# First-MLP tiles evicted in pairs from one bank, short score parts of two queries' blocks in shared banks, and a new order behind job 60

## The chip, the cores and the metric

The kernel runs on one core of a Trainium2 chip. The metric is the device time of one execution in microseconds (us); of several runs the median is given. The engines are TensorE (PE; its weight loads are shown as PEld), VectorE (DVE), ScalarE (ACT), GpSimd (POOL) and SyncE (SP, which here only issues DMAs). Matmuls write to PSUM, which has 8 banks of 512 fp32 values in each of 128 partitions.

## What is computed

Two branches are added to the input x of 2048 tokens by 512, both on the layer-normed x.

```
xn = layernorm(x)                          # 2048 x 512
# branch A: 32 heads of 16, 4 segments of 512 tokens
logits = q k^T / 4 + mask                  # within a segment
a_dot  = softmax(logits) v
a_mem  = (phi(q) M) / (phi(q) z + 1e-6)    # phi(t) = t+1 if t>0 else exp(t)
o      = g a_mem + (1-g) a_dot             # g = sigmoid(beta), per head
M, z  += phi(k)^T v, sum phi(k)            # for the next segment
A = o wo
# branch B: MLP with 1792 hidden units
B = gelu(layernorm(xn) w1 + b1) w2 + b2
out = x + A + B
```

## The kernel before

**Jobs.** The work is cut into some 1300 jobs. Each is a Python call that emits its instructions on all engines that it needs; an engine works through its own instructions in the order in which the jobs are emitted. `streams()` lists the jobs of each kind in their own fixed order; the string `ORDER` has one letter a job and says from which stream the next job comes. So `ORDER` fixes the order of every engine's queue, the DMA queue of SP included. It was made outside of this file. The string `BANKS` has one digit for each PSUM tile, in the order in which the jobs ask for them: `dense()` takes the next digit and returns that bank whole (128 x 512 fp32). Semaphores between the engines follow from the tiles: who takes a bank waits for the last reader of its earlier content.

**Groups.** A group i (0 to 15) is one segment of 512 tokens and 8 heads. Its jobs are:

- `T` (L495): q or k projected, 12 matmuls of 128x512; the halves are written to DRAM and read back in another layout (qst, kst).
- `M` (L636, L643): row maxima of the scores. For each t of 4 (two heads each) and each query block of 128 there are scores of up to 512 keys in two banks, one for each of two heads, by pairs of matmuls on the two halves of the array (48 rows each). VectorE adds the mask and takes the maximum straight from PSUM, one reduction and one read of its accumulator for each bank and block. The parts of a t are: block 3 (512 keys), blocks 2 and 0 (384 and 128 in one bank), block 1 (256). Each part is a job: 12 for a group.
- `R` (L514, L653 to L659): the maxima are transposed, split into halves of fp16, written to DRAM (md) and read back as two more rows of qst.
- `S` (L676, L681, L690): scores again, transposed, with the maximum taken off by these rows (50 rows); ScalarE takes exp from PSUM, POOL masks the diagonal blocks.
- `pv`, `PV` (L705): probabilities times v, with 32 columns of the array each, four at a time; `O` (L729 to L741) normalizes in three steps, over DVE, ACT and POOL.
- `N`, `K`, `Z`, `Qd`, `Q`: the memory branch (transposes of phi(k), products with v, phi(q) times the memory, its normalization).

**MLP.** It is cut into 16 jobs' worth j: 256 tokens (half hf of a segment) by one half of the hidden units (fh, 7 tiles of 128). `D` (L495 with w1s, L771): one tile of 128 hidden units by 256 tokens, 12 matmuls, then one VectorE instruction that scales it by a column and by a row `srow` into hT. `G` (L778): gelu of all seven tiles, on ScalarE, after a load of its table. `H` (L785 to L787): splits them into halves of fp16. `e` (L812, L818): the second layer, 14 jobs of 6 matmuls on the halves of the array, into two banks. `out` (L830, L833): the output projection of 128 tokens.

`V` projects v, `X` and `Xt` are the layer norm and its transposes, `wl`, `wm`, `wf` and `ws` load, measure, scale and split the weights in the first 80 us, `warm` (L843) is 8 matmuls of no use that keep PE busy; there are 14.

The names that the prediction speaks of are written with their indices: T(1,0) is q of group 1, S(7,3,1) the second score job of t = 3 of group 7, Q(15) the normalization of group 15's memory part, H(15,3) the last split of MLP job 15.

Of the kernel before, what the change touches and what calls it, by code (L numbers as in the profile page):

```python
# [14 lines left out]
OP = mybir.AluOpType  # L15
# [4 lines left out]
P = 128  # L20
D = 512
KT = D // P
# [9 lines left out]
FH = FT // 2  # L32
# [69 lines left out]


ORDER = (
    "atacctcaetcttetcawvavcatwvcaxeacatxvdccwvxwfttyyyxbxyyuxgyyyzozoywouoxyccyzhoAzzAootAAppciiizAznpBiiABfBncAiBpi"
    "gzBszniipnzBiimchqqqiCBqBqiiioAoACBCCBCjjqiojqAjqjcioijoiCikskkBcmDskioBjiqiqCjjoijqCiqjsCqjDiftaoCCpgkkkpkjqCj"
    "oloojjljoloojiipkkkkiqihspqijqqipqijqiqjsjqqjaajfgpiiqkkkkmpliqqiooiqpDlqoDopohijjiojiijpolsjiqaqajqiqiqqiiqapk"
    "akmkktspaqijqiqjqiqajqbqajopijjgDfopkkkDkjjjlooooDlhjjjolqiqqiipkkkkjiqqijqqjjiqiqjjqiqiqiDkkkkmpliilfnplimpngr"
    "rmrjjponijqjqjinjipiskmkkmkaiijrijjoojiqsjqqjiqiiiqqkkkkihlqlfmlogojqjqjqqjjasoojmkkkkmqjiqjqjjaojjpipmooisikkk"
    "klpilhiofmgoooqiqpppqiqiqqqiiiqqpsosmoiqqiiqiqppsslooijqjojijojijoiaakkkkmpaijqjqjaqqqjiqqjiqjqiikmkkakbqiaqqah"  # L110
    "lolfqjjojqmjgjjoolmmkkkkmhjjoojjiitjiojiippkkkkliiilnfnimpligniinipmrrijjrsijqjqiqjiqjqiipkmkkksiqjqijqjqjiqjqi"
    "iqjqikmpkkkiprlqsphlfojmjgopjjlojpjoomokmkkkqiqisjojiqisjqiqijqqijqhiqqiiqjsqiiqppmkkkkilalofomqpgopaoooospmlaj"
    "qqqjqqjqjqiiqiqqqjqiqqipipooooiijooppoiaakkkkmajiqpisqqjiqjqjaiqaqhjqqqjqaaqmkkkkbjlfoljqjmjgojjqolmkkkkmmjjjoo"
    "jjioijoiiippkpkkkiinliifniiilnnimlgrpmjjrmjjjrrijikkpskkiqqijqiqijqqjiqjiqjqiqjiqiispqkpkskksqilqoplfojmjgjjjpo"
    "ooojolmkkkkiqjiqpsjiqiqijqjqiqijqjiqiqiqiiqqkksmkpikplolfjjqmjgjjjoooooklpkmkkjiiopjqiqijqjiqpjqiqijqiqqiqiiqik"
    "kpspkkqiplpoooopljjjqqqjqjjqooolkpskmkpkmqqqpqjpjqqqjqjqpqqjqjqqqkmkkkqlllqqqqqqqqqrrrr"
)

BANKS = (
    "050123614061756123401632157467410534702651305176254301741260523716405142730612547306651240651024615024612504612"
    "504650124650412650412650412650142650142650421607653420107642531076425031702531270531270531270132570132570132576"
    "135402761350427163054273106542736574326574326537425632754632574631072456310724563071245360712453620731620731067"
    "203617621073621073621073621037621037621037261702361475023671540263701524603175246031746013746013713460713471630"
    "471630463714067314056723410523674105236741052367410527410527410527410527410527140352671450326475103264751023674"
    "523674523647253647236547236475264735264107532410765324107265431067512043675120436751204736152047361520473615270"
    "346150312750317250317253107250371257013275027135027134650132754062751340621375460376054370567403056374065374065"
    "307645307645307642153076241076241076241076253410762534621075346210754316024310264310432610432610324610324612403"
    "246013752640163754207156437120564371205647312056473120564731206547321065473265104723607423460273460273642073642"  # L130
    "073642051736420157642031765420316750316705315631705630157630157630157306173504621357462017345620147536210436024"
    "136024316403216403216403216403216740536740536740536740536271406"
)


# [14 lines left out]
def infini_mixer_kernel(ctx: ExitStack, tc: tile.TileContext, x, wq, wk, wv, wo, beta, w1, b1, w2, b2, out):  # L150
# [15 lines left out]
    def dense():  # L166
        return dps.tile([P, 512], F32, name="ps" + next(bank), bufs=1)
# [52 lines left out]
    def col(j):  # L220
        return sc[:, j:j + 1]
# [210 lines left out]
    srow = {}  # L432
# [192 lines left out]
    mc = cst.tile([P, 96], F32, name="mc")  # L625

    def m_jobs(i):
        def f(t, qbs):
            def go():
                ps = dense(), dense()  # L630
                o = 0
                for qb in qbs:
                    n = P * (qb + 1)
                    for b, p in enumerate(ps):
                        r = slice(64 * b, 64 * b + KM)
                        T.matmul(p[:, o:o + n], stk[i, 0][r, t, P * qb:P * qb + P], stk[i, 1][r, t, :n],  # L636
                                 start=True, stop=True)
                    o += n
                o = 0
                for qb in qbs:  # L640
                    n = P * (qb + 1)
                    for b, p in enumerate(ps):
                        V.tensor_tensor_reduce(p[:, o:o + n], p[:, o:o + n], mask[:, 512 - n:], 1.0, -3e38,  # L643
                                               OP.add, OP.max, mc[:, 16 * b + 4 * t + qb:16 * b + 4 * t + qb + 1])
# [114 lines left out]
    def d_jobs(j):  # L759
        hf, fh = divmod(j, 2)  # L760
        hs, hh = divmod(hf, 2)
        own = slice(256 * hh, 256 * hh + 256)
        hz = hzs[fh]

        def f(fi):
            def go():
                fo = FH * fh + fi
                p = dense()
                split3(p[:, :256], ((WT["1"], lambda w, k, a: w[:, fo, a, P * k:P * k + P]),
                                    (xnT[hs], lambda t, k, a: t[:, k, a, own])), KT, True, True)  # L770
                V.scalar_tensor_tensor(hz[:, fi, :], p[:, :256], col(F1 + fh), srow[hs][:, own], op0=OP.mult, op1=OP.mult)  # L771
            return go
        return [f(fi) for fi in range(FH)]

    def gelu(j):
        for f in range(FH):
# [149 lines left out]
```

## Time and profile before

| | before |
|---|---|
| median of 3 runs | 691.06 us (690.85 to 691.38) |
| the profiled execution | 691.51 us |
| its span, first to last instruction | 689.8 us |
| granted TensorE clock | 0.999 |

A profile line of a group reads: line of the kernel, engine, operation, output <- inputs, shape, count | busy us, mean ns of one | idle us before it, and what ended that. Matmuls are pipelined: the record of one runs on while the next has begun, so PE's idle time shows only where it was longer than this. In the chain that ended last, each piece is followed back from the last instruction to what released it.

The shape of a matmul line is rows*columns of the array that it uses, then the output. 128*128 is the whole array; 48*128, 50*128 and 64*128 are one of its halves; 128*32 is a quarter of its columns.

### The profile page before, as it was taken

The page shows a single profiled execution, that of the slowest core. Times are in us where ns is not written, and L with a number is a line of the kernel's source. Part 1 is how long each engine was busy: PE and PEld are TensorE (multiplying, and loading weights), DVE is VectorE, ACT ScalarE, POOL GpSimd, SP SyncE. Part 2 cuts the span into 40 slices and gives each one's busy share as a digit, 9 for nine tenths or more (in the row PEclk, how much of TensorE's full clock was granted, in tenths as well). Part 3 has the DMA queues.
Part 4 walks back from the last instruction along what each step waited for, and adds up shares of the span by engine and source line. Part 5 has one row for each costly group of instructions (what it writes and reads, how often), then busy time and mean ns, then how long its engine had stood idle before and what let it go on. Part 6 is the DMA issues. An engine that isn't in the chain of part 4 may idle for free.

```text
span 689.8 us, 17163 instructions
## 1 busy us (share of the span) xinstructions
PE 681.8 (99%) x6465; PEld 399.8 (58%) x6465; DVE 545.7 (79%) x1740; ACT 502.9 (73%) x972; POOL 340.5 (49%) x526
## 2 busy tenths in 40 slices
PE   8999999999999999999999999999999999999997
PEld 7855655565654546566554557567564456656653
DVE  6999968897795887998797787888688696969442
ACT  4486897788786659856794796766795687878870
POOL 5355567456535334663435355454353545446752
PEclk9999999999999999999999999999999999999999
DMA  9856342421203322421213224231120415140101
GB/s 277 249 149 201 92 109 49 117 55 31 65 24 102 94 67 45 122 50 33 69 26 98 58 73 100 72 86 32 41 72 24 132 19 154 17 109 2 19 1 62
DMA packets 51792, 55.15 MB, mean 80 GB/s; under 512 B 4782, under 2 KB 40636, under 8 KB 51708
## 3 DMA queue, kind: packets, MB, share of 16 engines
q1 hardware_dynamic: 49404, 49.84, 24.9%
q0 software_dynamic: 2304, 4.20, 3.8%
q8 instruction: 51, 0.84, 0.5%
q14 instruction: 33, 0.27, 0.1%
HBM read 36.99 MB, written 17.04 MB: 78 GB/s over the span
## 4 chain that ended last, share of the span: by engine, by line
PE 85%; DVE 5%; ACT 5%; DMA 2%; POOL 1%; issue 1%; SPq 0%; POOLq 0%; DVEq 0%; ACTq 0%
PE ps L495 36%; PE ps L812 17%; PE ps L705 10%; PE ps L830 6%; PE ps L676 5%; PE ps L636 5%; DVE ps L643 3%; ACT pt L681 2%; PE ps L586 2%; PE ps L514 1%; PE ps L843 1%; PE ps L321 1%; DMA wks<-in_A_wk_dram 1%; DMA qd<-hl 1%; PE ps L617 1%
## 5 line engine op out<-in xcount | busy, mean ns | idle before, releaser
L643 DVE CUSTOM_DVE_ANT_0 ps<-ps,mask 128x512 f32<-128x512 f32 (+3 forms) x512 | 233.9, 523 | 14.1 <-PE ps L636 12.9
L681 ACT ACTIVATE pt<-ps,qkcs 128x512 f32<-128x512 f32 (+1 forms) x384 | 206.8, 624 | 37.3 <-PE ps L676 35.2
L812 PE MATMUL ps<-w2s,hT 64*128 64x512 f16 x1344 | 176.6, 375 | 0.1
L495 PE MATMUL ps<-xnT,w1s 128*128 128x256 f16 x1344 | 158.0, 273 | 0.0
L690 POOL TENSOR_SCALAR_AFFINE_SELECT pt<-pt 128x256 f32<-128x256 f32 x256 | 101.0, 421 | 98.2 <-ACT pt L681 97.2
L495 PEld LDWEIGHTS <-w1s 128*128 128x128 f16 x1344 | 127.2, 98 | 28.5 <-issue 11.6
L787 POOL TENSOR_TENSOR hT<-hh,hT 128x512 f16<-128x512 f32 x64 | 67.7, 1057 | 86.3 <-ACT hT L786 82.7
L812 PEld LDWEIGHTS <-hT 64*128 64x128 f16 x1344 | 76.3, 94 | 49.8 <-issue 5.9
L705 PE MATMUL ps<-pt,vt 128*32 128x512 f32 (+3 forms) x1024 | 77.1, 435 | 0.1
L771 DVE SCALAR_TENSOR_TENSOR hT<-ps,sc,sr 128x256 f32<-128x256 f32 x112 | 52.4, 478 | 26.9 <-PE ps L495 26.7
L643 DVE DVE_READ_ACCUMULATOR2_ANT mc<- 128x1 f32 x512 | 71.0, 139 | 0.0
L636 PE MATMUL ps<-kst,qst 48*128 48x256 f16 (+3 forms) x512 | 66.7, 297 | 1.1 <-DMA qst<-qd 0.3
L676 PE MATMUL ps<-qst,kst 50*128 50x512 f16 (+3 forms) x512 | 66.2, 297 | 0.0
L786 ACT ACTIVATE hT<-hh 128x512 f16<-128x512 f32 x64 | 36.6, 572 | 33.3 <-POOL hh L785 32.9
L705 PEld LDWEIGHTS ps<-pt,vt 128*32 128x32 f32 x1024 | 30.5, 109 | 43.0 <-issue 32.4
L785 POOL TENSOR_SCALAR hh<-hT,sc 128x512 f32<-128x512 f32 x64 | 42.2, 660 | 25.7 <-ACT hT L778 24.1
L735 POOL TENSOR_TENSOR nN<-nN,oT 128x512 f32<-128x512 f32 x16 | 20.3, 1269 | 61.1 <-DVE oT L561 61.1
L778 ACT ACTIVATE hT<-hT,b1t 128x256 f32<-128x256 f32 x112 | 46.5, 495 | 0.2
L495 PE MATMUL ps<-xnT,wqs 128*128 128x512 f16 x192 | 44.2, 380 | 0.0
L495 PE MATMUL ps<-xnT,wks 128*128 128x512 f16 x192 | 44.1, 379 | 0.0
L495 PE MATMUL ps<-wvs,xnT 128*128 128x512 f16 x192 | 44.0, 379 | 0.0
L830 PE MATMUL ps<-wos,oT 128*128 128x512 f16 x192 | 43.3, 379 | 0.6 <-POOL oT L741 0.6
(225 smaller groups left out, 883.1 us busy)
## 6 DMA issues: line engine op xcount, KB each, us to landing
kd<-hl SPq DMA_DIRECT2D x48, 128.0 KB
qd<-hl SPq DMA_DIRECT2D x48, 128.0 KB
kst<-kd SPq DMA_DIRECT2D x32, 192.0 KB
qst<-qd SPq DMA_DIRECT2D x32, 192.0 KB
acc<-in_A_x_dram SPq DMA_DIRECT2D x16, 256.0 KB
acc<-in_B_b_dram POOLq DMA_DIRECT2D x16, 256.0 KB, 4.2
out_dram<-acc SPq DMA_DIRECT2D x16, 256.0 KB
xt<-in_A_x_dram SPq DMA_DIRECT2D x14, 256.0 KB
```

Of the source, the lines that this page charges most:

```text
L495: T.matmul(p, wsl(ws, k, a), xsl(xs, k, b), start=s0 and i == 0, stop=s1 and i == 3 * n - 1)
L636: T.matmul(p[:, o:o + n], stk[i, 0][r, t, P * qb:P * qb + P], stk[i, 1][r, t, :n], start=True, stop=True)
L643: V.tensor_tensor_reduce(p[:, o:o + n], p[:, o:o + n], mask[:, 512 - n:], 1.0, -3e38, OP.add, OP.max, mc[:, 16 * b + 4 * t + qb:16 * b + 4 ...
L676: T.matmul(p[:, o:o + n], stk[i, 1][r, t, P * kb:P * kb + P], stk[i, 0][r, t, P * kb:], start=True, stop=True)
L681: A.activation(e[:, OFF[kbs[0]]:OFF[kbs[0]] + o], p[:, :o], AF.Exp, scale=qkcs[:, 1, i % NG:i % NG + 1])
L690: G.affine_select(v, v, pattern=[[0, 2], [1, P]], compare_op=OP.is_ge, fill=0.0, base=0, channel_multiplier=-1)
L705: T.matmul(p[32 * c:32 * c + 32, P * kb:], vt[s, kb][:, 4 * g + c, 16 * odd:16 * odd + 32], pt[i, 2 * c + odd][:, OFF[kb]:OFF[kb] + LEN[kb ...
L771: V.scalar_tensor_tensor(hz[:, fi, :], p[:, :256], col(F1 + fh), srow[hs][:, own], op0=OP.mult, op1=OP.mult)
L778: A.activation(z, z, AF.Gelu_apprx_tanh, bias=b1t[:, FH * (j % 2) + f:FH * (j % 2) + f + 1])
L787: G.tensor_tensor(hT[:, z, 1, :], t, hT[:, z, 0, :], op=OP.subtract)
L812: w = T.matmul(pes[j][a], hTs[fh][r, fi, u, P * a:P * a + P], w2s[r, fo, v, :], start=n == 0 and m == 0, stop=fi == FH - 1 and m == 2, ski ...
L830: T.matmul(p, o[:, u, P * b:P * b + P], wos[:, g, v, :], start=i == 0, stop=i == 3 * NG - 1)
```

## The change

It has three parts.

1. `D`: tiles of hidden units go in pairs. Two tiles of 128x256 are accumulated one behind the other into the two halves of one bank, and one VectorE instruction of 128x512 scales both, with the row `srow` repeated for each. The seventh tile stays alone. So 7 jobs for each j become 4, 112 become 64.
2. `M`: the parts of 256 keys (block 1) of two t's share their two banks: of 12 jobs for a group, 10 are left. The number of matmuls and reductions stays.
3. `ORDER` and `BANKS` are new: the first 60 jobs are the same as before; behind them the order differs everywhere, and there are 1228 jobs, where there were 1308, and 1061 bank tiles, where there were 1173. The kinds of the other jobs and their numbers stay.

```diff
-        maxi += [("M", i, n) for n in range(12)] + [("R", i)]
+        maxi += [("M", i, n) for n in range(10)] + [("R", i)]
...
-        hid += [("D", j, f) for f in range(FH)]
+        hid += [("D", j, f) for f in range(0, FH, 2)]
...
-        def f(t, qbs):
+        def f(ts, qbs):
             def go():
                 ps = dense(), dense()
+                todo = [(t, qb) for t in ts for qb in qbs]
                 o = 0
-                for qb in qbs:
+                for t, qb in todo:
                     n = P * (qb + 1)
...
-                for qb in qbs:
+                for t, qb in todo:
                     n = P * (qb + 1)
                     for b, p in enumerate(ps):
                         V.tensor_tensor_reduce(p[:, o:o + n], p[:, o:o + n], mask[:, 512 - n:], 1.0, -3e38,
...
-        return [f(t, q) for t in range(4) for q in ((3,), (2, 0), (1,))]
+        return [f(t, q) for a in (0, 2) for t, q in (((a,), (3,)), ((a,), (2, 0)), ((a + 1,), (3,)), ((a + 1,), (2, 0)), ((a, a + 1), (1,)))]
...
-                fo = FH * fh + fi
-                p = dense()
-                split3(p[:, :256], ((WT["1"], lambda w, k, a: w[:, fo, a, P * k:P * k + P]),
-                                    (xnT[hs], lambda t, k, a: t[:, k, a, own])), KT, True, True)
-                V.scalar_tensor_tensor(hz[:, fi, :], p[:, :256], col(F1 + fh), srow[hs][:, own], op0=OP.mult, op1=OP.mult)
+                n = min(2, FH - fi)
+                p = dense().rearrange("p (n c) -> p n c", n=2)[:, :n, :]
+                for a in range(n):
+                    fo = FH * fh + fi + a
+                    split3(p[:, a], ((WT["1"], lambda w, k, u: w[:, fo, u, P * k:P * k + P]),
+                                     (xnT[hs], lambda t, k, u: t[:, k, u, own])), KT, True, True)
+                V.scalar_tensor_tensor(hz[:, fi:fi + n, :], p, col(F1 + fh), srow[hs][:, own].unsqueeze(1).broadcast_to([P, n, 256]),
+                                       op0=OP.mult, op1=OP.mult)
             return go
-        return [f(fi) for fi in range(FH)]
+        return {fi: f(fi) for fi in range(0, FH, 2)}
```

Four places of the orders, written out as jobs (only those with work on PE unless said otherwise; the index of M counts its new parts in the new order). In the old order D(8,4) is one tile; in the new one D(8,4) is the pair of tiles 4 and 5.

```
groups 7 and 8
  old: N(8) S(7,1,0) S(7,1,1) D(8,4) D(8,5) S(7,1,2) S(7,3,0) M(8,0) M(8,1) warm S(7,3,1) M(8,2) D(8,6) S(7,3,2) M(8,3) M(8,4) pv(7,1,0)
  new: S(7,1,0) S(7,1,1) D(8,4) S(7,1,2) S(7,3,0) M(8,0) M(8,1) K(7) S(7,3,1) N(8) M(8,2) S(7,3,2) M(8,3) pv(7,1,0)
from R(15) to S(15,0,0), H and O (not on PE) shown too
  old: H(14,1) O(14,0) H(14,2) D(15,0) D(15,1) D(15,2) D(15,3) H(14,3) O(14,1)
  new: e(13,9) H(14,2) O(14,0) e(13,10) D(15,2) H(14,3)
the end, from the last pv on, Q, O and H shown too
  old: pv(15,1,0) Q(15) pv(15,1,1) pv(15,1,2) PV(15,1) e(15,4) O(15,0) O(15,1) O(15,2) e(15,5) ... e(15,13) out(3,0)
  new: pv(15,1,0) pv(15,1,1) pv(15,1,2) PV(15,1) e(15,1) H(15,3) e(15,2) ... e(15,5) Q(15) O(15,0) O(15,1) e(15,6) ... e(15,10) O(15,2) e(15,11) e(15,12) e(15,13) out(3,0)
the load of the second half of w2 (1.28 MB) among SP's DMAs
  old: T(1,1) V(0,1) load T(1,0)
  new: D(0,2) load D(0,4) ... T(1,1) T(1,0)
```

More of the change, by code (lines that the diff above doesn't have):

```diff
@@ new lines @@
+    "jiaqjqpibfDgkDkkkDjjoaDjljpqjmlooojiqqiilkpkkkpiqqjiqjqiqjjqihqqjiqjqiikkpkkmlqilfmngnnjljjanprjjirijkmkskkiijo"
+    "ijsjriijprjiqjqiqikkpkkqiplmlhqfmjgojqljqmjoomjsqihqijkkkkjjaojqjiqjqiqjiqkppkkklomploqimfpgpoipqqqipqqsiqpsiqq"
+    "oiqiiqipmosjjqqqilojjisojiqaqjpsikakkkmajqaqqjjqiqjqijqiqjkiaqbaqhqakmkkjjloljjfjmglojkmkkkqjjojjiimjhijikkkmpk"
+    "liilnfilmipgnnppoiqirpimnrjiqjqijqjqijqqisjmkkkkijrjiqqjjqmiqhqjijqqpsaiikkkpkrispllofmjgopjjmoojqsqjqjqiqiikkk"
+    "lpkmqisjqhqijqjqimsjqjqiqqijpkpkkkliilooimfpgotospjqpjqajqqjqlqqijiqqqjqiimppipqooiikkkkiqpajqiooaapqqsjiqqjaja"
@@ L128 @@
[L128 to L132, printed above, removed]
+    "050123614061756123401632157467630251467130652471210376524103726541650214650124650126045126012412546012546012564"
@@ L133 @@
+    "061451206451026452106542016542104652175360342154763602157436046573045674305637045637045673150274631502631502361"
+    "506231506321506321503621503062153062153746052157340612753407621534025761360547245103672643510672435106724531067"
+    "204167204106724016072461074253170364251706341706341370641730463170416317034167130471670341706370324610735610753"
+    "61075361075367105367175536571036751036214034612030634216034251"
 )
```

30 lines of the change are left out of this document (12 added, 18 removed).

## The prediction, made before the result

> **What bounds the kernel now.** I read the page's busy shares first, then its chain that ended last, then the table by stretches of 100 us, the waits of PE, and last the timelines of PE, ACT and DVE at the places that the change moves.
>
> ```profile
> span 689.8 us, 17163 instructions
> PE 681.8 (99%) x6465; PEld 399.8 (58%) x6465; DVE 545.7 (79%) x1740; ACT 502.9 (73%) x972; POOL 340.5 (49%) x526
> ...
> PE 85%; DVE 5%; ACT 5%; DMA 2%; POOL 1%; issue 1%; SPq 0%; POOLq 0%; DVEq 0%; ACTq 0%
> ...
> 100.00:200.00 100.00, 99.87 (x1063) 62.01 (x1062) 84.69 (x287) 82.58 (x166) 55.35 (x89) 1.00 0.23 62
> ...
> 500.00:600.00 100.00, 99.80 (x875) 55.48 (x877) 80.52 (x256) 76.56 (x141) 49.42 (x80) 1.00 0.28 72
> 600.00:690.00 90.00, 85.20 (x762) 48.31 (x754) 51.14 (x140) 58.50 (x107) 45.71 (x67) 0.99 0.14 37
> ```
>
> The stretches' columns are window, length, then busy time of PE, PEld, DVE, ACT and POOL. TensorE is the bound in every stretch: of 100 us it shows 99.8 busy. It is idle 8.0 us in all (689.8 - 681.8), and 4.8 of these lie in the last 90. VectorE and ScalarE are free for 21 and 27% of the time. Yet they hold 5% each of the chain, 34.5 us each: there a matmul was released only just in time. The change alters no matmul. So it can pay only through waits of PE, most of them too short to be seen as idle time, and through the order in which PE meets its jobs.
>
> What one job costs PE is read from the chain in order of time, start and length of a run, and from PE's timeline:
>
> ```profile
> 99.86 4.04 PE ps L495 x36
> ...
> 131.00 2.73 PE ps L495 x24
> ...
> 135.21 1.42 PE ps L495 x12
> ...
> 302.96 0.38 PE L676 MATMUL ps<-qst,kst 50*128 50x512 f16 x2
> 303.18 0.81 PE L812 MATMUL ps<-w2s,hT 64*128 64x512 f16 x6
> 303.83 0.38 PE L676 MATMUL ps<-qst,kst 50*128 50x384 f16 x4
> 304.14 1.48 PE L495 MATMUL ps<-xnT,w1s 128*128 128x256 f16 x12
> 305.56 0.28 PE L676 MATMUL ps<-qst,kst 50*128 50x256 f16 x2
> 305.68 0.38 PE L636 MATMUL ps<-kst,qst 48*128 48x384 f16 x4
> 305.90 0.52 PE L676 MATMUL ps<-qst,kst 50*128 50x512 f16 x2
> ```
>
> Each further D job (12 matmuls of L495) adds 1.31 us, and a run of them .11 once. An e job is .65 (303.18 to 303.83), a 512-wide score pair .22 (302.96 to 303.18), a 256-wide pair .12. A job of 384 and 128 takes .22 where the next one is also of half height (305.68 to 305.90) and .31 where a full-height D follows (303.83 to 304.14). So a change of array shape costs about .1 us, either way; D after D, or score after score, costs nothing.
>
> **The change part by part.**
>
> ```profile
> L771 DVE SCALAR_TENSOR_TENSOR hT<-ps,sc,sr 128x256 f32<-128x256 f32 x112 | 52.4, 478 | 26.9 <-PE ps L495 26.7
> L818 DVE SCALAR_TENSOR_TENSOR acc<-ps,sc,acc 128x512 f32<-128x512 f32 x32 | 22.5, 743 | 7.1 <-PE ps L812 6.9
> L643 DVE CUSTOM_DVE_ANT_0 ps<-ps,mask 128x256 f32<-128x256 f32 x128 | 53.1, 455 | 1.9 <-PE ps L636 1.9
> L643 DVE DVE_READ_ACCUMULATOR2_ANT mc<- 128x1 f32 x512 | 71.0, 139 | 0.0
> ```
>
> *Paired D tiles.* 112 evictions of 478 ns become 48 of twice the width and 16 single ones. The nearest row to a 512-wide one is L818, the same operation from PSUM with three operands: 743 ns. DVE loses 48 x (2 x 478 - 743) = 10.2 us of 545.7, 1.9%. If the repeated row operand slowed it, the far end is 2 x 478 each and nothing is saved. DVE is not the bound; 1.9% of its 34.5 us on the chain is .65, so bounds 0 and -2, and I take **-.5**. The cover is PE's other jobs, which go on meanwhile.
>
> The Trainium skill, page "TensorEngine Tiling (Array Packing)", section PSUM Bottleneck, advises to vectorize PSUM access across tiles in the same bank. By it, with eviction as the limit, all 10.2 us would come off (681); the trace, with DVE at 79% and PE at 99%, does not bear this out.
>
> *Banks.* 48 + 64 = 112 bank handovers go. But a bank is held per pair for 24 matmuls and one eviction, 2.62 + .74 = 3.4 us, where two banks were held 1.31 + .48 each, 3.6 together. The merged maxima hold two banks for two queries' parts: four reductions of 455 + 139 = 2.4 us on DVE, where each part held them 1.2. Bank time is the same, DVE's work for the maxima too: **0** of itself, either way.
>
> The Trainium skill, "PSUM — Partial Sum Buffer", section PSUM bank collisions raise a hardware error, says to guard PSUM by bank, since an engine may not read a bank that another writes. By it the first half of a pair cannot be evicted under the second; it speaks for the nought, and no run here tries an overlap.
>
> *The order.* Read off as jobs, the old order changes array shape 232 times, the new one 223 times: 9 x .1 = **-.9** (-.8 to -1).
>
> *Head.* The first 60 jobs stand. Behind them SP has the 1.28 MB load of the second half of w2 before the writes of q and k for group 1, where it had it between them.
>
> ```profile
> 54.90 5.37 DMA qd<-hl
> 60.69 3.80 DMA qst<-qd
> ...
> w2s<-in_B_w_dram SPq DMA_DIRECT2D x1, 1280.0 KB
> ...
> 40.00:60.00 20.00, 19.68 (x143) 9.27 (x144) 19.83 (x71) 13.90 (x28) 11.12 (x13) 1.00 0.52 161
> ...
> 48.88 0.50 PE L636 MATMUL ps<-kst,qst 48*128 48x256 f16 x4 [0.32 <-DVE mc L643]
> ...
> 64.54 0.60 PE L636 MATMUL ps<-kst,qst 48*128 48x512 f16 x5 [0.34 <-DMA qst<-qd]
> ```
>
> Without that load beside it the write of qd should land sooner than in 5.37 us, and the .34 goes. Against it, from T(1,0) to M(1,0) PE has 12.5 us of work in the new order and 13.2 in the old, added up by such job times. The two waits seen are .66 together; 1.5 more or less are the ends, and I take **-.5**. Other weight steps move too (splits of w1 and w2 to DVE, POOL and ACT); DVE is busy for 19.83 of the 20 us from 40 to 60, so a gain there is not sure.
>
> *Tail.*
>
> ```profile
> 666.87 0.69 DVE L560 TENSOR_TENSOR rc<-rc,rt 128x512 f32<-128x512 f32 x1 [3.39 <-ACT rt L556]
> 667.60 0.69 DVE L561 SCALAR_TENSOR_TENSOR rc<-rc,rt 128x512 f32<-128x512 f32 x1
> 668.26 0.75 DVE L718 SCALAR_TENSOR_TENSOR nN<-ps,bg,nN 128x512 f32<-128x512 f32 x1
> ...
> 674.55 2.67 PE L830 MATMUL ps<-wos,oT 128*128 128x512 f16 x11
> 677.85 8.16 PE L830 MATMUL ps<-wos,oT 128*128 128x512 f16 x37 [0.63 <-POOL oT L741]
> ```
>
> Before the last output tiles PE waits .63 for the last head's oT. In the new order 13 e jobs, not 10, follow the last pv job (+1.95 us of cover); the two steps of Q(15) on DVE (1.4 us) move behind that head's first step, where before they delayed it by about .9. Net cover +1.4, so the wait goes: **-.7** (-.9 to +.9, if e jobs wait for H(15,3)).
>
> *A tight spot.* At groups 7 and 8 the old order had a dummy warm-up (L843) and a D job between the score jobs:
>
> ```profile
> 345.00 0.60 PE L676 MATMUL ps<-qst,kst 50*128 50x512 f16 x6
> ...
> 349.62 1.05 PE L843 MATMUL ps<-ones 128*128 128x256 f16 x8
> ...
> 346.59 5.70 ACT L681 ACTIVATE pt<-ps,qkcs 128x512 f32<-128x512 f32 x10
> ```
>
> The new order puts N(8) right behind S(7,3,1), in a bank that this one has just filled. From S(7,1,0) to N(8) PE has 4.8 us of work (one pair of D 2.62, seven short score jobs 1.4, K and four changes of shape .8 by estimate). ACT must first do nine exponentials of .57 (5.70 / 10), 5.1 us, and began them 1.59 after PE here. That gives 6.7, a wait of 1.9; if ACT begins at once, .3. Before, such waits were .3 there. N(8)'s wait stops what is queued behind it on PE: M(8,2), S(7,3,2) and the last pv of group 7. I take **+1.2** (0 to +2).
>
> *Shorter leads.* Maxima go R to DRAM and back before the S jobs:
>
> ```profile
> 601.14 0.26 PE L514 MATMUL ps<-ident,mc 64*96 64x64 f32 x2
> ...
> 602.07 0.30 SPq L656 DMA_DIRECT2D md<-mhl  x1
> ...
> 603.47 0.53 SPq L659 DMA_DIRECT2D qst<-md  x2
> ...
> 605.69 0.61 PE L676 MATMUL ps<-qst,kst 50*128 50x512 f16 x6
> ```
>
> The first write took until 603.47, 1.40; with as much for the second the way is 602.07 - 601.14 + 1.40 + .53 + 1.40 = 4.3 us, longer where ACT or DVE lag; here PE came after 4.55. In the new order the work between R and S is 3.9 to 4.8 us in seven of the 16 groups (for 15: two e jobs and one pair of D, 1.3 + 2.6), in the old one in one group outside the head. Ends 0 and +4, seven times 0 to .6; as the queues' lag is unknown I take **+1.0**. All other leads could as well be better: -1.5.
>
> **Sum:** -.5 - .9 - .5 - .7 + 1.2 + 1.0 = -.4. The profiled execution took 691.5 (span 689.8 and 1.7 around it), the median of the runs is 691.06, .45 less. So 691.1 for a profiled one and **690.7 as a median**.
>
> **The rivals.** *Faster, the waits thin out.* DVE and ACT hold 69 us of the chain; in pieces of about .6 these are some 115 hand-offs, each of which can hide up to .15 us, since a matmul's record runs on that long into the next: up to 17 us. If lighter DVE work and deeper banks took a quarter of it, 4.3 us would go: 686.8. For: 112 handovers less. Against: the same bank time, and leads that are shorter, not longer. *Slower, the leads are too short.* Where R to S, or a bank's next use, comes below the way of 4.3 us or the eviction, PE waits and nothing makes it up. Decisive is whether ACT and DVE lag at R: at .3 us a group nothing is felt, from .6 on it outweighs the gains. At the upper ends, 2.0 for the spot and 4 for the leads, with the other gains: 691.06 - 2.6 + 6 = 694.5. *The wide eviction isn't shorter:* 2 x 478; only the .5 is lost, 691.2.
>
> **How the numbers follow.** About .2%, 1.4 us, is what a measurement can tell here from no change. No change, 689.7 to 692.4, with my 690.7: .37, the third rival among it. Faster: .34. Slower: .29. The range leaves the ends of both: the low end is 686.6, just under the first rival; the high end 695.2, a little over the second.
>
> **What would show it.** L771 at x48 of 512 near 743 ns and DVE near 535 us busy: step one. PE busy time unchanged to 2 us, and L843 still x14. No idle time at L830 for oT: the tail. Idle time of PE at L514 (N) near 348: the tight spot. Waits of L676 for qst<-md: the leads. Wrong would be a DVE that gets idle while PE still waits for L643, or head jobs that start later by more than 1.5 us at 100 us.

## The result and the profile after

The changed kernel took 697.8 us (median; 696.2 to 699.0) against 691.1 for the kernel before on the same chip: 1.0091 times as long, 95% interval 1.0076 to 1.0105. It is 6.7 us slower, where 0.4 faster was forecast; the time lies above the forecast's high end of 695.2. One execution of pairs_rebanked, below, ran at a granted clock of .59 and took 1107 us; no figure here holds it.

The page's head after, busy time and share of each engine, and the shares of the chain that ended last:

```profile
span 696.5 us, 17147 instructions
...
PE 682.9 (98%) x6465; PEld 389.0 (56%) x6465; DVE 538.8 (77%) x1692; ACT 503.2 (72%) x972; POOL 342.1 (49%) x526
...
PE 72%; DVE 11%; ACT 6%; DMA 5%; issue 2%; POOL 2%; SPq 1%; POOLq 0%; DVEq 0%; ACTq 0%
```

The span grew by 6.7 us, PE's busy time by 1.1, and DVE's fell by 7.0. PE thus does the same work and stands idle more. In the chain PE gives up 13%; DVE takes 6 of these and DMA 3. Next the table by stretches, columns as before; two rows of the kernel before, then the same stretches after:

```profile
400.00:500.00 100.00, 100.00 (x1011) 61.87 (x1006) 79.75 (x248) 73.36 (x147) 48.83 (x72) 1.00 0.27 69
...
600.00:689.80 89.80, 85.20 (x762) 48.31 (x754) 51.14 (x140) 58.50 (x107) 45.71 (x67) 0.99 0.14 37
```

```profile
400.00:500.00 100.00, 98.60 (x1010) 59.39 (x1004) 78.79 (x251) 74.01 (x146) 50.30 (x75) 1.00 0.28 68
...
600.00:696.50 96.50, 89.12 (x800) 47.55 (x794) 55.11 (x146) 63.57 (x117) 48.50 (x72) 0.99 0.15 40
```

The stretch from 400 to 500, where PE had no idle time before, now has 1.4 us; the last one has 7.4 (before 4.6 up to the span's end). What PE waited for is in the view of waits: total us, times, longest one.

```profile
PE ps L676 <- DMA qst<-md: 2.3, 1, 2.3
...
PE ps L636 <- DMA qst<-qd: 1.5, 3, 0.6
...
PE ps L833 <- POOL oT L741: 0.6, 1, 0.6
PE ps L513 <- DVE mc L643: 0.6, 3, 0.3
PE ps L513 <- ACT pt L681: 0.3, 1, 0.3
```

The largest new wait is for maxima on their way through DRAM (qst<-md): 2.3 us, once. Before, PE had no such row at all; the waits for DVE stay small.

Since waits shorter than a matmul's record do not show as idle time, I also took from each trace, for all matmuls, by how much each starts later than uninterrupted runs of the same shapes let it (.095 us for a change of array shape counted as work). Below this sum is called **PE's waits**. Before it is 33.3 us with 234 changes of shape, after 40.8 with 225: +7.5 - 9 x .095 = +6.6, the growth of the span. (The .095 is put in, from the rows of the prediction; it is not measured by this sum.) Four jobs hold 5.8 of the 7.5 (their waits after, less those before): S(15,0,0) 2.55, M(11,0) 1.67, N(8) .98, S(2,0,0) .55. The rest is spread. The profiled execution after is the slowest of the four, 698.95 us, so these waits are at the upper end of what the kernel shows.

### The profile page after: what moved, and what is told of

Read it like the earlier page. It is cut to its first block, busy times and chain, and to the rows that moved or that the text cites. A ratio compares the mean times of both kernels' runs of the same rounds, so it can differ in the third digit from the quotient of the medians.

```text
span 696.5 us, 17147 instructions
## 1 busy us (share of the span) xinstructions
PE 682.9 (98%) x6465; PEld 389.0 (56%) x6465; DVE 538.8 (77%) x1692; ACT 503.2 (72%) x972; POOL 342.1 (49%) x526
## 4 chain that ended last, share of the span: by engine, by line
PE 72%; DVE 11%; ACT 6%; DMA 5%; issue 2%; POOL 2%; SPq 1%; POOLq 0%; DVEq 0%; ACTq 0%
PE ps L494 31%; PE ps L815 13%; PE ps L705 7%; PE ps L833 6%; DVE ps L643 5%; PE ps L676 5%; PE ps L636 4%; ACT pt L681 3%; DMA qst<-qd 2%; DMA qd<-hl 2%; PE ps L585 1%; PE ps L513 1%; DVE mc L643 1%; PE ps L846 1%; DMA md<-mhl 1%
## 5 line engine op out<-in xcount | busy, mean ns | idle before, releaser
L643 DVE CUSTOM_DVE_ANT_0 ps<-ps,mask 128x384 f32<-128x384 f32 (+3 forms) x512 | 234.1, 523 | 21.7 <-PE ps L636 18.6
L690 POOL TENSOR_SCALAR_AFFINE_SELECT pt<-pt 128x256 f32<-128x256 f32 x256 | 103.7, 429 | 119.7 <-ACT pt L681 118.8
L494 PE MATMUL ps<-xnT,w1s 128*128 128x256 f16 x1344 | 155.1, 273 | 0.2 <-DVE mc L643 0.2
L815 PEld LDWEIGHTS <-hT 64*128 64x128 f16 x1344 | 67.1, 94 | 57.0 <-issue 4.8
L705 PE MATMUL ps<-pt,vt 128*32 128x256 f32 (+3 forms) x1024 | 77.1, 436 | 0.0
L773 DVE SCALAR_TENSOR_TENSOR hT<-ps,sc,sr 128x512 f32<-128x512 f32 x64 | 43.2, 680 | 29.2 <-PE ps L494 28.7
L636 PE MATMUL ps<-kst,qst 48*128 48x128 f16 (+3 forms) x512 | 61.9, 297 | 1.9 <-DMA qst<-qd 1.5
L705 PEld LDWEIGHTS ps<-pt,vt 128*32 128x32 f32 x1024 | 31.3, 109 | 40.5 <-issue 31.5
L676 PEld LDWEIGHTS <-kst 50*128 50x128 f16 x512 | 25.2, 94 | 32.7 <-issue 17.3
```

Of the source, the lines that this page charges most:

```text
L494: T.matmul(p, wsl(ws, k, a), xsl(xs, k, b), start=s0 and i == 0, stop=s1 and i == 3 * n - 1)
L676: T.matmul(p[:, o:o + n], stk[i, 1][r, t, P * kb:P * kb + P], stk[i, 0][r, t, P * kb:], start=True, stop=True)
L690: G.affine_select(v, v, pattern=[[0, 2], [1, P]], compare_op=OP.is_ge, fill=0.0, base=0, channel_multiplier=-1)
L705: T.matmul(p[32 * c:32 * c + 32, P * kb:], vt[s, kb][:, 4 * g + c, 16 * odd:16 * odd + 32], pt[i, 2 * c + odd][:, OFF[kb]:OFF[kb] + LEN[kb ...
L773: V.scalar_tensor_tensor(hz[:, fi:fi + n, :], p, col(F1 + fh), srow[hs][:, own].unsqueeze(1).broadcast_to([P, n, 256]), op0=OP.mult, op1=O ...
L815: w = T.matmul(pes[j][a], hTs[fh][r, fi, u, P * a:P * a + P], w2s[r, fo, v, :], start=n == 0 and m == 0, stop=fi == FH - 1 and m == 2, ski ...
```

## The experiments

The ratio is to the kernel before, run on the same chip, with its 95% interval. PE's waits are those of the profiled execution.

| run | us | ratio | PE's waits |
|---|---|---|---|
| changed kernel | 697.8 | 1.0091 [1.0076, 1.0105] | 40.8 |
| ops_old_order | 718.8 | 1.0391 [1.0376, 1.0407] | 61.5 |
| merge_only | 703.0 | 1.0161 [1.0144, 1.0178] | 44.9 |
| pairs_only | 710.5 | 1.0256 [1.0238, 1.0273] | 53.8 |
| adjacent_pairs | 698.5 | 1.0095 [1.0078, 1.0112] | 39.8 |
| old_ops_new_order | 791.6 | 1.1457 [1.1414, 1.1499] | 135.4 |
| lumps_old_ops | 746.1 | 1.0780 [1.0748, 1.0813] | 92.2 |
| narrow_evictions | 698.0 | 1.0087 [1.0066, 1.0108] | 40.5 |
| late_readers | 698.8 | 1.0101 [1.0086, 1.0116] | 40.9 |
| fetch_clear | 694.7 | 1.0048 [1.0034, 1.0061] | 37.3 |
| fetch_hit | 696.5 | 1.0071 [1.0058, 1.0085] | 38.9 |
| before_clear | 692.0 | 1.0005 [0.9996, 1.0014] | 34.2 |
| rebanked_before | 692.9 | 1.0019 [1.0010, 1.0028] | 34.0 |
| adjacent_rebanked | 693.4 | 1.0025 [1.0015, 1.0036] | 35.4 |
| clear_rebanked | 695.2 | 1.0052 [1.0038, 1.0066] | 37.9 |
| clear_rebanked_n8 | 696.4 | 1.0068 [1.0054, 1.0081] | 39.6 |
| ops_rebanked | 716.0 | 1.0340 [1.0324, 1.0356] | 59.6 |
| pairs_rebanked | 710.6 | 1.0259 [1.0237, 1.0282] | 54.2 |
| lumps_rebanked | 715.9 | 1.0348 [1.0331, 1.0365] | 58.3 |

The time follows PE's waits in every run. In six of them these waits are not all idle time, for a matmul that runs at a lower clock makes the next one late too. Outside of the first 8 and the last 5 us the granted clock is .5 for stretches of 3.4 us, once each in ops_rebanked and pairs_only, twice in pairs_rebanked and lumps_rebanked; lumps_old_ops and old_ops_new_order have some 34 us of it each. At half speed 3.4 us do the work of 1.7. The other runs have no such stretch, the kernels before and after among them.

### The width of the eviction

`narrow_evictions`: the changed kernel, each shared bank emptied by two evictions of 256 instead of one of 512.

```diff
-                V.scalar_tensor_tensor(hz[:, fi:fi + n, :], p, col(F1 + fh), srow[hs][:, own].unsqueeze(1).broadcast_to([P, n, 256]),
-                                       op0=OP.mult, op1=OP.mult)
+                for a in range(n):
+                    V.scalar_tensor_tensor(hz[:, fi + a, :], p[:, a], col(F1 + fh), srow[hs][:, own], op0=OP.mult, op1=OP.mult)
```

> The changed kernel with its order and banks, but each shared bank is emptied by two evictions of 256 columns instead of one of 512. The prediction's term for the wide eviction, -.5 us, says 698.0 to 698.6 us. Rival 'wide eviction' as a cost: 697 us or less.

698.0 us against 697.8 for the changed kernel: the intervals of the two ratios lie over each other. The groups of the eviction by form, of the changed kernel first:

```profile
L773 DVE SCALAR_TENSOR_TENSOR hT<-ps,sc,sr 128x512 f32<-128x512 f32 x48 | 35.7, 746 | 23.3 <-PE ps L494 22.8
...
L773 DVE SCALAR_TENSOR_TENSOR hT<-ps,sc,sr 128x256 f32<-128x256 f32 x16 | 7.7, 481 | 5.9 <-PE ps L494 5.9
```

and of narrow_evictions:

```profile
L774 DVE SCALAR_TENSOR_TENSOR hT<-ps,sc,sr 128x256 f32<-128x256 f32 x112 | 49.2, 478 | 27.8 <-PE ps L494 26.1 <-POOL pt L690 0.9
```

The wide form takes 746 ns, where twice the narrow one is 956. DVE is busy for 544.2 us in narrow_evictions, 538.8 after. In both the eviction mostly stands idle before it, waiting for PE.

The equal times don't show that the width is worth nothing, though. Both kernels run the same matmuls in the same order, and their traces can be laid side by side: narrow_evictions is .3 us early at 26 us, 1.5 late at 636, and then gains 2.1 at S(15,0,0), which in the changed kernel waits for a late write of maxima (below) and here hardly does:

```profile
644.53 0.33 SPq L656 DMA_DIRECT2D md<-mhl  x1
645.95 0.55 SPq L659 DMA_DIRECT2D qst<-md  x2
...
647.54 0.83 PE L676 MATMUL ps<-qst,kst 50*128 50x512 f16 x2 [0.20 <-DMA qst<-md]
```

Without this luck the narrow evictions would have taken some 1.7 us more in this pair of traces. Some of that stands at other waits for DMA (.5 at M(1,0), .3 at M(11,0)), so it is an upper end. The runs of each kernel lie about 3 us apart; they can't tell the forecast .5 from nothing or from 1.7.

### The edits without the new order

Each of these keeps the old sequence of jobs and puts a pair or a merged part at the place of its second part; the other first parts fall away. Banks are those of the parts that stay.

- `ops_old_order`: both edits. `merge_only`: the maxima alone. `pairs_only`: the 48 pairs alone. `adjacent_pairs`: only the 31 pairs between whose tiles no other matmul stood.
- `old_ops_new_order`: the new order with the old single tiles and parts side by side. `lumps_old_ops`: the old order and single tiles, 29 first tiles moved beside their partners.

```diff
-        hid += [("D", j, f) for f in range(0, FH, 2)]
+        hid += [("D", j, f) for f in range(FH) if (j, f - 1) not in PAIRED]
...
-                n = min(2, FH - fi)
+                n = 1 + ((j, fi) in PAIRED)
```

(The difference of adjacent_pairs to the changed kernel's code; in the others whole edits are left out.)

> Both new operations (paired D tiles, merged maxima) put into the old order, each pair or merged job at the place of its second part, old banks. Theory 'order' (the new order brings readers too soon behind what they wait for, the operations cost nothing): 690.0 to 692.0 us, PE waits as before, DVE some 9 us less busy. Rival 'operations' (a bank shared by two tiles and a wide eviction in VectorE's queue make PE wait): 695 us or more, with PE waiting for L643 and L773 all along.

> Only the merged maxima, in the old order with the old banks, D as before. Theory 'order': 690.5 to 692 us, VectorE as busy as before (545 us). Rival 'operations', if it is the maxima that hold banks too long: 693 us or more, with PE waiting for L643.

> The old order with all 48 pairs, each at the place of its second tile, maxima as before. With both operations the old order took 718.8 us, with the merged maxima alone 703.0; if the two add up this one takes 706 to 708 us. Theory 'order': the cost is that of the 29 tiles that are moved. Rival 'wide eviction': it is that of the evictions; the kernel with 31 adjacent pairs then shows most of it.

> The old order, and only those 31 pairs of D tiles share a bank and one wide eviction that already stand side by side on PE there; maxima as before. PE's order is unchanged. Theory 'order' (the operation is neutral, its place counts): 690.0 to 691.8 us, VectorE about 6 us less busy. Rival 'wide eviction' (a bank held for two tiles and a wide instruction in VectorE's queue make PE wait): 693 us or more.

> The new order with the old operations: each pair of D is two jobs of one tile, each merged maximum two jobs, side by side at the place of the one, the second with another free bank. Theory 'order': 696 to 700 us, with the waits at S(15,0,0), M(11,0) and N(8) still there. Rival 'operations': back to 690 to 692 us.

> Old operations and old order, but the 29 tiles of D whose partner stands apart are moved beside it (15 of them with another bank), each with its own bank and its own narrow eviction. Theory 'order': the same 700 to 710 us as with all pairs at these places, since PE loses the work that lay between its score jobs. Rival 'wide eviction': 691 to 694 us, since every eviction is as before.

Five of the six came out slower than the theory 'order' allowed, and pairs_only slower than the 706 to 708 of a plain sum. The edits in the old order cost 27 us together, 11 (maxima) and 19 (pairs) alone. With its own order and banks the changed kernel gives back 21 of these 27; what it still loses is looked for below. The last two runs are inconclusive: the tiles that they add took banks by a simple rule, and single waits of up to 6.1 us, for a reduction of M or an exponential that has still to empty the bank, stand in front of tiles in their traces (D(6,2) in lumps_old_ops, D(2,1) with 3.9 in old_ops_new_order). So the new order with the old edits was never measured under banks that suit it. In adjacent_pairs, where no matmul moves, the new waits stand at the pairs: D(14,1) 1.32, D(13,2) 1.10, D(2,1) 1.01. The pair uses the bank of its second tile, and asks for it one tile, 1.3 us, earlier than that tile did.

### Banks dealt out anew

To part the banks from the order, I walked through the jobs with the durations and release times of before's trace and gave each job the bank that comes free first (the first 110 jobs keep theirs). `rebanked_before` does this to the kernel before alone; `adjacent_rebanked` and `ops_rebanked` do it to two of the kernels above.

> The kernel before, all jobs and their order as they were; only the PSUM banks behind the first 110 jobs are dealt out anew, each job taking the bank that a walk over the trace of before says is released first (503 of 1173 or so change). It is the control for the next run. If such a dealing is as good as the old one: 689 to 692.5 us, PE's waits as before (33 us) or 1.5 us less. If the old banks hold knowledge that the walk lacks: 695 or more.

> As adjacent_pairs (old order, 31 pairs of D tiles that stood side by side share a bank and one wide eviction, 698.5 us) but with banks dealt out as in rebanked_before. Theory (a pair costs nothing of itself, the 7 us came from banks that were not yet free where the pair starts): within 1 us of rebanked_before. Rival (a shared bank is held longer, and that itself costs): 695 us or more, with waits of .5 to 1.3 us again at D(14,1), D(13,2), D(2,1), D(8,4).

> ops_old_order (both edits of the evictions, old order of jobs, 718.8 us) with its banks dealt out anew as in rebanked_before. If the evictions as such cost nothing and all of the 27 us came from banks: 691 to 694 us, as rebanked_before. If jobs that are moved to where their pair is need an order of their own, as the walk says (4.8 us more wait than in rebanked_before): 695 to 700 us. If longer holds cost by themselves: 705 or more.

The control is 1.35 us slower than before (just above the 692.5 expected; 941 of its 1173 digits differ, not some 503): the deal is almost as good as the old one. With it, 31 pairs in a shared bank cost .55 us, and the 6.6 us of adjacent_pairs are gone: a shared bank costs nothing much of itself, a bank that is not yet free does. But both edits in the old order stay at 716 us, only 3 less than with the old banks. The walk, which foresaw 4.8 us more wait than for the control, missed some 20. The 716 lies where the expectation put a cost of longer holds. For the pairs the next section looks at that; for the merged maxima no such run was made. In merge_only PE waits for reductions of VectorE before transposes (L513) nine times, 3.3 us in all, and before M (L636) six times, 2.2 us, where the kernel before has .3; whether the held banks or the moved parts do this stays open.

### The hole that a moved tile leaves

`pairs_rebanked` and `lumps_rebanked` move the same 29 tiles to the same places and deal the banks out anew; the first has shared banks and wide evictions, the second the old single ones.

> pairs_only (all 48 pairs of D tiles in one bank at the place of the second tile, maxima as before, old order otherwise, 710.5 us) with its banks dealt out anew as in rebanked_before. If the loss is one of order, a tile moved away from its place no longer covers a wait there: 703 to 710 us, and lumps_rebanked within 3 us of it. If it is one of banks: 692 to 696.

> The kernel before with its old single evictions and one bank a tile; 29 first tiles are moved beside their partners, to the same places as in pairs_rebanked, and the banks are dealt out anew. Theory (order: the moved tile leaves a hole): 702 to 710 us, within 3 us of pairs_rebanked. Rival (the shared bank and the late first half are what costs): 692 to 696 us, some 10 below pairs_rebanked.

The old evictions are as slow, even slower: 715.9 against 710.6. They are not within the 3 us that I had expected; one wait of T(7,1), for a bank that an eviction of D still reads, makes up most of the gap. It leads the view of PE's waits of lumps_rebanked:

```profile
PE ps L495 <- DVE hT L771: 3.5, 1, 3.5
```

The rival (10 below) falls: for the pairs it is the move that costs, not the shared bank or the wide eviction. One place where it can be seen, PE's timeline of before:

```profile
161.98 0.43 PE L676 MATMUL ps<-qst,kst 50*128 50x512 f16 x2
162.35 1.48 PE L495 MATMUL ps<-xnT,w1s 128*128 128x256 f16 x12
163.76 0.26 PE L514 MATMUL ps<-ident,mc 64*96 64x64 f32 x2
163.86 0.49 PE L676 MATMUL ps<-qst,kst 50*128 50x384 f16 x6
164.28 2.76 PE L495 MATMUL ps<-xnT,wqs 128*128 128x512 f16 x12
```

and the same jobs in lumps_rebanked, where the tile D(4,0) has gone to its partner behind T(4,1):

```profile
168.74 0.44 PE L676 MATMUL ps<-qst,kst 50*128 50x512 f16 x2
169.04 0.26 PE L514 MATMUL ps<-ident,mc 64*96 64x64 f32 x2
169.56 0.32 PE L676 MATMUL ps<-qst,kst 50*128 50x384 f16 x1 [0.25 <-DVE acc L818]
170.54 0.60 PE L676 MATMUL ps<-qst,kst 50*128 50x384 f16 x4 [0.67 <-DVE xnT L477]
171.64 0.27 PE L676 MATMUL ps<-qst,kst 50*128 50x256 f16 x1 [0.49 <-DVE mhl L654]
```

The score job S(2,3,1) followed the tile of 1.48 us without a gap; without the tile it and its neighbour wait .25 + .67 + .49 = 1.41 us, three times for DVE. The tile had been the cover. What comes next costs as much again: the projection behind these waits, 12 matmuls, takes 4.41 us, where it took 2.76 before. From 171.8 on, for 3.4 us, the granted clock is .5 (third column from the right in the row of a stretch, below the projection's line):

```profile
171.84 4.41 PE L495 MATMUL ps<-xnT,wqs 128*128 128x512 f16 x12
...
172.00:173.00 1.00, 1.00 (x3) 0.30 (x2) 0.00 (x0) 1.00 (x4) 1.00 (x3) 0.50 0.07 15
```

In pairs_rebanked the clock falls at the same job, and once more in each near 80 us: up to 3.4 us of the loss in both. One execution of pairs_rebanked had a granted clock of 1.000 and took 708.1 us; the two with .995 and .994 took 711.2 and 710.6. What sets the clock down is not tested here.

So the loss of lumps_rebanked against rebanked_before, 23 us, or 24.3 by PE's waits, has three parts that can be named: waits at score jobs (S: 3.7 us in rebanked_before, 14.3 in lumps_rebanked), T(7,1) 3.5, the lower clock up to 3.4. Some 7 us are spread. That the score jobs lost their cover was followed at one place; for the others it is argued from the equal loss with either eviction.

### Late maxima: packets of instructions

This is the wait of 2.3 us at S(15,0,0). PE's timeline of the changed kernel, then the issues on SP's queue:

```profile
641.52 0.26 PE L513 MATMUL ps<-ident,mc 64*96 64x64 f32 x2
641.62 1.46 PE L815 MATMUL ps<-w2s,hT 64*128 64x512 f16 x12
643.01 2.79 PE L494 MATMUL ps<-xnT,w1s 128*128 128x256 f16 x24
648.08 0.69 PE L676 MATMUL ps<-qst,kst 50*128 50x512 f16 x2 [2.27 <-DMA qst<-md]
```

```profile
642.91 0.33 SPq L656 DMA_DIRECT2D md<-mhl  x1
646.54 0.55 SPq L659 DMA_DIRECT2D qst<-md  x2
```

The lead is the two e jobs and the pair of D of the prediction, 4.2 us from 641.6 to 645.8. The write of md, however, took 3.63 us, not 1.40. Three windows of the DMA view show why, its lines of queues with packets, MB and share. First 642.91 to 644.00, then 644.00 to 645.50, then 645.50 to 645.70:

```profile
q1 hardware_dynamic: 75, 0.02, 6.3%
```

```profile
q8 instruction: 1, 0.02, 6.2%
q14 instruction: 1, 0.01, 2.0%
```

```profile
q1 hardware_dynamic: 5, 0.00, 5.4%
```

75 of the write's 80 packets pass in the first window. Then a packet of instructions of 16 KB starts at 644.05 and takes 1.48 us by the DMA records, and only when it has ended, from 645.52 on, do the last five packets of the write pass. In groups 2, 4 and 10 it is alike: there too the write's last packet ends .1 us after a packet of instructions. The whole trace holds 50 such packets (that of before 51) for 6465 matmuls, one for each 127 to 129. If these are PE's instructions, more matmuls at the start move them against the work:

```diff
-        for _ in range(8):
-            T.matmul(p[:, :256], w[:, :P], w, start=True, stop=True)
+        u = P if n <= 10 else 2 * P
+        for _ in range(2048 // u):
+            T.matmul(p[:, :u], w[:, :P], w[:, :u], start=True, stop=True)
```

(`fetch_clear`; `fetch_hit` has `n <= 8`, `before_clear` 36 more matmuls in the kernel before.)

> The changed kernel, in which eleven of the fourteen warm-ups (those in the head) make their 2048 columns as 16 matmuls of 128 instead of 8 of 256: 88 more matmuls in the instruction stream, the same columns. This moves the 16 KB instruction packets of the DMA trace, one for each 128 matmuls, against the work: by their old places none falls into the 1.4 us of a write of maxima (now 4 do: groups 2, 4, 10, 15). Theory (a packet beside the write delays it, and the late maxima hold the scores): the writes take 1.4 to 1.8 us for 2, 4, 10 and 15, the wait at S(15,0,0) falls from 2.56 to under .6, the time by 2 to 4 us, to 694 to 696 us. Rival (packet and late write only met by chance; queues' lag is the cause): S(15,0,0) still waits 2 or more, 697 to 698.5 us.

> The same with nine of the warm-ups in halves, 72 more matmuls. By their old places the packets now fall into the writes of groups 5, 6, 11 and 14 and into none of 2, 4, 10, 15. Theory: the writes of 5, 6, 11 and 14 take 2 to 3 us, those of 2, 4, 10 and 15 1.4 to 1.8; the wait at S(15,0,0) is gone, and where the lead of 5, 6, 11 or 14 is short a wait of up to 1.5 us stands instead: 695 to 699 us, above fetch_clear by 0 to 4. Rival: as the changed kernel, 697 to 698.5, with S(15,0,0) waiting 2 or more and the same four writes slow.

> The kernel before with 36 more matmuls in the warm-ups of the head (four of them 16 of 128 columns, one 8 of 128 and 4 of 256), so that by its old places no packet falls into a write of maxima. Theory (its leads are long enough to hide a late write: no wait over .2 at the first score of a group behind the head): within .6 us of before. Rival (halved warm-ups are a gain of their own, or packets cost elsewhere too): 1.5 us or more below before.

The time from the write of md to the issue behind it, in us, by group:

| | 2 | 4 | 6 | 10 | 12 | 14 | 15 |
|---|---|---|---|---|---|---|---|
| changed kernel | 2.45 | 2.57 | 1.39 | 3.08 | 2.59 | 1.40 | 3.63 |
| fetch_clear | 1.74 | 1.44 | 2.47 | 1.40 | 2.38 | 1.47 | 1.42 |
| fetch_hit | 2.81 | 1.44 | 2.80 | 1.40 | 3.84 | 2.54 | 1.42 |

In fetch_clear the writes of 4, 10 and 15 are quick, S(15,0,0) waits .38, and the kernel takes 694.7, 3.1 us less: PE's waits are 3.5 less. In fetch_hit, 16 matmuls fewer, the packets meet 6, 12 and 14; S(6,0,0), S(12,0,0) and S(14,0,0) now wait .95, .66 and .71, and the time is 696.5, between the two. By group not all came true. In fetch_hit 5 and 11 stayed quick and 2 did not; in fetch_clear, where no write was to be hit, that of group 0 in the head was (2.93). And a packet of instructions is not the only cause of a late write: group 12's 2.4 to 2.6 in the first two rows, fetch_clear's 2.47 in group 6 and fetch_hit's 2.81 in group 2 have none among the write's own packets, but packets of 1024 or 2048 bytes of other transfers, still on their way. SP's queue of fetch_clear at group 15, where the write now takes 1.41:

```profile
641.51 0.33 SPq L656 DMA_DIRECT2D md<-mhl  x1
642.92 0.55 SPq L659 DMA_DIRECT2D qst<-md  x2
```

The 1.7 us at M(11,0) went with it: SP's queue runs in order, and behind the late md of group 10 stood the writes of q and k for group 11. SP's queue of the changed kernel, and of fetch_clear:

```profile
448.45 0.30 SPq L656 DMA_DIRECT2D md<-mhl  x1
451.53 0.53 SPq L659 DMA_DIRECT2D qst<-md  x2
...
459.51 0.79 SPq L541 DMA_DIRECT2D qst<-qd  x2
```

```profile
447.99 0.30 SPq L656 DMA_DIRECT2D md<-mhl  x1
449.39 0.53 SPq L659 DMA_DIRECT2D qst<-md  x2
...
457.03 0.79 SPq L541 DMA_DIRECT2D qst<-qd  x2
```

From md to the last issue it is 11.06 us in the one, 9.04 in the other. before_clear is as before (its interval holds 1): the halved warm-ups are no gain of their own. (Not all of its writes became quick: behind the head those of groups 5 and 8 take 2.35 and 2.56.) The old order has late writes too: in the trace of before that of group 3 takes from 164.99 to 167.33. Yet its S(i,0,0) behind the head wait .19 at most. Two projections of q and k and a D stand between.

### Mending the rest by hand

`late_readers`: the changed kernel, three e jobs each moved ahead of S(15,0,0) and M(11,0), to lengthen their leads. `clear_rebanked`: fetch_clear with banks dealt out from the changed kernel's own trace. `clear_rebanked_n8`: the same with N(8) behind M(8,2), S(7,3,2) and M(8,3). Only `ORDER` and `BANKS` are edited.

> The changed kernel, but six e jobs moved: e(13,11) to e(13,13) ahead of S(15,0,0), e(9,7) to e(9,9) ahead of M(11,0), 1.95 us more lead at each place; banks unchanged. Theory 'order': the waits there (2.56 and 1.68 us in the profile of the changed kernel) go or shrink below 0.7, 1 to 3.6 us less: 694.2 to 696.8 us. Rival 'operations': 697 to 698.5 us, the waits turn up at the next jobs.

> fetch_clear with its PSUM banks behind the first 110 jobs dealt out anew by a walk over the trace of the changed kernel (the bank released first). Order and evictions as in the changed kernel. If the rest of its loss lies in banks that come free late: 691 to 693 us, PE's waits 34 us or less. If it lies in the order (leads, head, spot): 694 to 696 us, waits 36 to 38, with N(8) at 1.0.

> As clear_rebanked, and N(8) stands behind M(8,2), S(7,3,2) and M(8,3) instead of directly behind S(7,3,1). Theory (N(8) stood in the queue of ACT behind nine exponentials, and all of PE with it): N(8) waits under .3, and the time is .5 to 1.0 us below clear_rebanked. Rival (what stood behind N(8) waits now in its place): within .4 us of clear_rebanked.

None helps. In late_readers the e jobs are missing where they stood: e(14,0) now waits 1.05 us, S(15,2,0) and M(11,3) .85 each, and the sum is unchanged. (Group 10's write happened to be quick in this trace, 1.40, and group 15's late, 3.14; so it says something of S(15,0,0), not of M(11,0).) The new banks leave the sum at 37.9. That does not clear the old ones: in this trace the write of group 13 takes 2.52, and its score jobs wait 1.2 us more than in fetch_clear, so a gain of about 1 us by the banks may be hidden behind it. With N(8) moved, it waits no more (.03), but M(8,3) waits 1.32 and S(7,3,2) .63 in its place. The spot is short of ACT and DVE work done in time for either order that was tried. No version beat the kernel before.

## Why the prediction was wrong, step by step

- **Shorter leads, +1.0: the step that failed.** The mechanism was right and its size was not: S(15,0,0) and S(2,0,0) gave 3.1 us, and M(11,0) 1.7 more through SP's queue. I built the way of 4.3 us on one quiet write of 1.40, took the late end of it to be lag of ACT and DVE, and gave seven groups a common small price. What came were a few large ones from packets of instructions; writes of 2.0 to 2.7 stood in before's trace already, hidden by its longer leads. The slower rival had the right sign and shape, and .29; the time went 3.3 us beyond its 694.5. That fetch_clear, with these writes quick, takes 694.7 is no proof of it but chance: the 694.5 holds 4 us for the leads, of which fetch_clear still pays about 1 (S(6,0,0) .6, S(15,0,0) .4).
- **Wide eviction, -.5:** the duration was right (746 ns for 743), the DVE time came off (7.0 us of 10.2), and what this was worth stays open: 697.8 and 698.0 us with the wide and the narrow form, but up to 1.7 us of gain by the two traces, which the luck of one write hides. The way to the number was unsound in any case: a share of the chain was turned into a rate of gain. The Trainium skill's advice to vectorize PSUM access (page "TensorEngine Tiling (Array Packing)", section PSUM Bottleneck) pays on the evicting engine here, 746 ns for two tiles instead of 956; the kernel's time shows no gain that could be told from the spread of the runs.
- **Banks, 0:** right for the pair by itself (.55 us for 31 pairs), but only with a bank that is free 1.3 us earlier. This condition was not in the text. For the merged maxima it stays open (11 us in the old order).
- **Changes of shape, -.9:** 225 for 234, nine fewer as counted, at .095 each by the rows before; no run shows this price by itself.
- **Head, -.5:** the write of qd landed sooner, and the read behind it later, as the chain after shows:

```profile
54.16 3.36 DMA qd<-hl
57.94 4.76 DMA qst<-qd
```

  Before it was 5.37 and 3.80. M(1,0) waits .52 for .59: nothing gained.
- **Tail, -.7:** the .6 for oT is still there. The cover grew, but DVE's steps, of the changed kernel, are these:

```profile
672.44 1.41 DVE L821 SCALAR_TENSOR_TENSOR acc<-ps,sc,acc 128x512 f32<-128x512 f32 x2
673.77 0.74 DVE L718 SCALAR_TENSOR_TENSOR nN<-ps,bg,nN 128x512 f32<-128x512 f32 x1
674.43 0.74 DVE L719 SCALAR_TENSOR_TENSOR nD<-ps,eo,nD 128x512 f32<-128x512 f32 x1
675.09 0.68 DVE L559 TENSOR_TENSOR rc<-rc,rt 128x512 f32<-128x512 f32 x1
675.80 0.69 DVE L560 SCALAR_TENSOR_TENSOR rc<-rc,rt 128x512 f32<-128x512 f32 x1
...
676.42 0.73 DVE L729 STREAM_SHUFFLE oT<-nD 128x512 f32<-128x512 f32 x1
```

  Q's two steps (L559, L560) moved behind L718 and L719, as I had it, but not behind the shuffle L729 that the head needs next, and two evictions of e now stand ahead of L718. What was to be saved is queued on DVE all the same.
- **Tight spot, +1.2:** right. N(8) waits 1.02 us by PE's waits, for DVE and ACT, as PE's timeline after shows:

```profile
350.46 0.27 PE L513 MATMUL ps<-ident,phk 64*128 64x64 f32 x1 [0.16 <-DVE mc L643]
351.08 0.46 PE L513 MATMUL ps<-ident,phk 64*128 64x64 f32 x7 [0.35 <-ACT pt L681]
```

The sum as it came out: changes of shape -.9, spot +1.0, leads +4.8, the others 0, and about +1.8 spread over the other jobs, 6.7 in all. The cause of these 1.8 is not known; what the wide eviction gained, if it did, is in them. The range had +4 for the leads against gains of 2.6 that were all counted on, and of which .9 came. The first rival, waits that thin out by lighter DVE work and save 4.3 us, falls: PE's waits grew, and 5.4 us of DVE work more or less moved them by 1.7 at most.

## What to carry to other kernels

Where the bound engine is 99% busy, each of its jobs is also the cover of someone's wait: before work is put together, look at what stood between its parts, since here 29 tiles moved to their partners cost 18 to 23 us, a lower clock behind the waits included, and the cheaper eviction repaid at most a small part. Price a hand-off through DRAM by its slowest instance in the trace, not by a quiet one, and let leads be longer than that. Do not turn an off-path engine's saved time into a share of the chain's gain. And before two kernels of equal time are called equal, look whether a hit or a miss of this kind stands in only one of the two traces.

## What the hardware showed unexpectedly

A packet of instructions of 16 KB (.9 to 1.5 us by the changed kernel's DMA records) comes for each 127 to 129 matmuls. Where one fell into a small write (16 KB in packets of 256 bytes), the write's last packets passed only after it: 1.40 us became 2.5 to 3.6 in four groups of the changed kernel. That it is DMA hardware which both share is read from the order of the packets, not shown by itself. Where it falls depends on the number of matmuls ahead: 16 of them (fetch_clear to fetch_hit) were worth 1.8 us of time. It is not the number alone: in narrow_evictions, with the same matmuls, the packet at group 15 starts .2 us after the last of the write's packets instead of ahead of its last five, and the write takes 1.42 instead of 3.63. That may also be why the runs of the changed kernel lie 2.7 us apart and those of the kernel before, on the same chip, .5; this was not tried.

The granted clock halved for stretches of 3.4 us behind places where PE had waited, for instance three times within 2.3 us in lumps_rebanked; each costs up to 1.7 us on top of the waits.
